# A gated linear attention and an MLP mixer on one core: queries and keys of two batches transposed by DMA, prefix sums with channels on partitions

## The chip, the core and the metric

One core of a Trainium2 chip. TensorE (PE) multiplies matrices into PSUM, which has eight banks of 128 partitions by 512 fp32 here; ScalarE (ACT) computes exponentials and copies, VectorE (DVE) elementwise operations, GpSimd (POOL) some elementwise work and the loads that change the type, and SyncE (SP) issues other transfers. Each engine runs its own queue in order and waits on semaphores for the others. The metric is the device time of one execution in microseconds; lower is better.

## The reference

The first half is an attention with a decaying state, by batch (4) and head (8), over 768 steps with a head size of 48:

```python
f = 1.0 / (1.0 + np.exp(-f_logit))
for t in range(S):
    state = f[:, :, t, :, None] * state + np.einsum('bhd,bhe->bhde', k[:, :, t], v[:, :, t])
    y[:, :, t] = np.einsum('bhd,bhde->bhe', q[:, :, t], state)
```

The second half is a mixer over the 768 steps and then over the 384 channels of `y`, with the heads put side by side as `x` (4 x 768 x 384):

```python
xt = x.transpose(0, 2, 1)
h = np.maximum(xt @ w_tok1, 0.0) @ w_tok2
u = x + h.transpose(0, 2, 1)
h2 = np.maximum(u @ w_ch1, 0.0) @ w_ch2
return (u + h2).astype(np.float32)
```

w_tok1 is 768 x 256, w_tok2 256 x 768, w_ch1 384 x 1536, w_ch2 1536 x 384. Inputs and output are float32.

## The kernel before, in words

**Attention in chunks.** A batch's 768 steps are six chunks of 128. With L = -log f, the prefix sum of L within a chunk is s; q is multiplied by exp(-s) and k by exp(s), and then the chunk is plain causal attention without a softmax, plus q times the state from the chunks before it. Steps lie on partitions, heads and channels on the free axis. In `gates` ScalarE makes L from the logits (L324, L325) and its high half as bf16 (L326), VectorE, or for batch 3 POOL, the low half (L329, L332). `attention` then does, for each chunk:

- `sums` on TensorE (L344 to L353): the prefix sums, as the triangle of ones times the high and then the low half (384 columns each), and eight matmuls of one column for the chunk's total by channel, which the last chunk doesn't need;
- two exponentials on ScalarE (L361, L363), and one of the totals (`glast`, L366);
- two products on VectorE (`qh`, L369, and `kh`, L371);
- eight transposes on TensorE of pairs of heads (L382) and one copy of the whole bank out of PSUM (`qkT`, L386), so that channels lie on partitions;
- `scores` (L396): eight matmuls with 48 contraction rows, in pairs on the upper and lower half of the array; VectorE masks them into `AmT` (L403);
- `parts` (L419): k times v for the new state, eight matmuls with 64 weight columns each, onto the upper or lower half of the partitions by the head's parity; the state is updated on VectorE (L426 to L431) and copied to a block-diagonal bf16 form, `state_bd` (L311 on ScalarE, L315 on POOL);
- `outs`: queries times the earlier state (L448) and masked scores times v (L455) in one bank, copied to `x_bf` and `x_nat`.

G, Gi, qh, kh, qkT, AmT, glast and state_bd have two buffers each, by the chunk's parity. f, k, q and v have three buffers each, by batch.

**Mixer.** For each batch `mixer` runs the token matmuls (L480, L492), adds the result into `x_nat` (L496), copies it to bf16 (`u_bf`), transposes it by 18 transposes on TensorE into six banks with six copies (`uT`, L508 and L513), and runs the channel matmuls: 72 of 384 columns for `w_ch1` (L524, each group of three followed by a relu on ScalarE or VectorE, L534 and L536), and 72 for `w_ch2` (L546), an add (L552), and an output store from SP (L555).

**Order.** Nothing is issued in the order of this text. `Plan` holds every operation with its dependencies, a rank and an estimated cost, and `order` walks through time: of all the operations that are ready it takes the one that can start first, and among equals the one of the lowest rank. That fixes the order of each engine's queue and the PSUM bank of each group; an operation that opens a bank waits for a free one. Ranks come from `due` (attention, L559) and `ranks` (mixer, L564): chunk c of batch 2 has rank 62 + 5c, of batch 3 101 + 5c; batch 2's `w_ch1` groups have 108 + 0.7n.

**Loads.** Loads on POOL keep the order in which they are written (L288 to L304, and L581): batch 0 by chunks, the four weights up to `w_ch1`, f of batch 1, chunks 0 and 1 of batch 1, `w_ch2`, the other chunks, then f, k, q and v of batch 2 whole, and of batch 3 whole. At most eight are in flight, and their rows must fit the descriptor ring.

Of the kernel before, what the change touches and what calls it, by code (L numbers as in the profile page):

```python
# [17 lines left out]
NBANK = 8  # L18
RING = 16384

# [19 lines left out]
class Plan:  # L40
# [40 lines left out]
    @staticmethod  # L81
    def cost(op, engine):

        what, *n = op.kind
        if what == "mm":
            return n[0], n[0] + 166
        if what == "el":
            free, psum, fast = n
            if engine == ACT:
                own = free / 1.2 + (67 if psum else 97)  # L90
                return own, own + 103
            if engine == DVE:
                own = free / (0.96 * fast) + 67
                return own, own + 83
            own = free * (1.2 if fast != 1.5 else 2.05) + 80
            return own, own
        return n[0], n[1]

    def order(self):
        for op in self.ops:  # L100
            first = op.before | ({op.behind} if op.behind else set())
            op.missing = len(first)
            for x in first:
                x.after.append(op)
        free = {e: 0.0 for e in (PE, ACT, DVE, POOL, SP)}
        ready = {e: [] for e in free}
        banks = [0.0] * NBANK
        wire = 0.0
        landed: list = []
        done = []  # L110

        def offer(op):
            t = max([x.end for x in op.before], default=0.0)
            if op.kind[0] == "load" and op.engines == (POOL,) and op.kind[3]:
# [3 lines left out]
                for at, rows in reversed(landed):  # L118
                    held += rows
                    if held > RING:  # L120
                        t = max(t, at)
                        break
            for e in op.engines:
                ready[e].append((t + (WAKE[e] if t else 0.0), op))

        for op in self.ops:
            if not op.missing:
                offer(op)
        while len(done) < len(self.ops):
            best = None  # L130
            for e, line in ready.items():
                for t, op in line:
                    if op.engine is not None:
                        continue
                    t = max(t, free[e])
                    if op.bank is not None and op.bank.at is None:
                        t = max(t, min(banks) + 55)
                    if best is None or (t, op.rank) < best[0]:
                        best = ((t, op.rank), e, op)
            (t, _), e, op = best  # L140
            ready[e] = [(a, o) for a, o in ready[e] if o is not op and o.engine is None]
            if op.bank is not None and op.bank.at is None:
                op.bank.at = min(range(NBANK), key=lambda j: banks[j])
                banks[op.bank.at] = math.inf
            own, till = self.cost(op, e)
            op.engine, op.start = e, t
            free[e] = t + own
            op.end = t + till
            if op.kind[0] == "load":
                size = op.kind[3]  # L150
                if size:
                    wire = max(wire, t + 1700) + size
                    op.end = wire + 1100
                if size and e == POOL:
                    landed.append((op.end, op.kind[2]))
            if op.bank is not None:
                op.bank.users -= 1
                if not op.bank.users:
                    banks[op.bank.at] = op.end
            done.append(op)  # L160
            for x in op.after:
                x.missing -= 1
                if not x.missing:
                    offer(x)
        return sorted(done, key=lambda o: o.start)
# [7 lines left out]
def kernel(  # L173
# [21 lines left out]

    sb = ctx.enter_context(tc.tile_pool(name="sb", bufs=1))
# [15 lines left out]
    q_sb = [st([128, H, NCH, D], BF16, f"q_sb{i}") for i in range(NB)]  # L212
    k_sb = [st([128, H, NCH, D], BF16, f"k_sb{i}") for i in range(NB)]
    v_sb = [st([128, H, NCH, D], BF16, f"v_sb{i}") for i in range(NB)]
    f_sb = [st([128, H, NCH, D], FP32, f"f_sb{i}") for i in range(NB)]
    Lhi = [st([128, NCH, H, 64], BF16, f"Lhi{i}") for i in range(2)]
    Llo = [st([128, NCH, H, 64], BF16, f"Llo{i}") for i in range(2)]
    G = [st([128, H, D], BF16, f"G{i}") for i in range(2)]
    Gi = [st([128, H, D], BF16, f"Gi{i}") for i in range(2)]
    qh = [st([128, H, 64], BF16, f"qh{i}") for i in range(2)]  # L220
    kh = [st([128, H, 64], BF16, f"kh{i}") for i in range(2)]
    qkT = [st([128, 8, 128], BF16, f"qkT{i}") for i in range(2)]
    AmT = [st([128, 8, 128], BF16, f"AmT{i}") for i in range(2)]
    glast = [st([128, HP], FP32, f"glast{i}") for i in range(2)]
    state = st([128, HP, D], FP32, "state")
    tsum = st([128, HP, D], FP32, "tsum")
    state_bd = [st([128, HP, 2 * D], BF16, f"state_bd{i}") for i in range(2)]
# [5 lines left out]
    uT = st([128, 3, S], BF16, "uT")  # L233
# [11 lines left out]
    names = {"f": (f_sb, f_logit), "k": (k_sb, k), "q": (q_sb, q), "v": (v_sb, v)}  # L245

    def load(what, b, c=None, engine=POOL):
        for n in what:
            dst, src = names[n]
            into = dst[b % NB] if c is None else dst[b % NB][:, :, c, :]  # L250
# [5 lines left out]
                make=[(n, b % NB, j) for j in (range(NCH) if c is None else (c,))],  # L256
# [25 lines left out]
    for i in range(2):  # L282
        for n, tl in (("L", Lhi[i]), ("L", Llo[i])):
            once(DVE, lambda tl=tl: nc.vector.memset(tl[:, :, :, D:64], 0.0), [("L", i, c) for c in range(NCH)], 400)
        for n, tl in (("qh", qh[i]), ("kh", kh[i])):
            once(DVE, lambda tl=tl: nc.vector.memset(tl[:, :, D:64], 0.0), [(n, i)], 120)
        once(DVE, lambda i=i: nc.vector.memset(state_bd[i], 0.0), [("sbd", i)], 220)
    for c in range(1, NCH):  # L288
# [10 lines left out]
    load("kqv", 1, 0)  # L299
    load("kqv", 1, 1)  # L300
    load_w("w_ch2", w_ch2, moe_w_ch2, 5600)
    for c in range(2, NCH):
        load("kqv", 1, c)
    load("fkqv", 2)  # L304
# [13 lines left out]
    def gates(b, c, r):  # L318
        fb = f_sb[b % NB][:, :, c, :]
        hi = Lhi[b % 2][:, c, :, 0:D]  # L320
        lo = Llo[b % 2][:, c, :, 0:D]
        key, lk = ("f", b % NB, c), ("L", b % 2, c)
# [12 lines left out]
    def attention(b, c, r):  # L335
        i, nb = c % 2, b % NB
        last = c == NCH - 1
        hi_c, lo_c = Lhi[b % 2][:, c], Llo[b % 2][:, c]
        lk = ("L", b % 2, c)

# [3 lines left out]
        def sums():  # L344
            pm = banks[p_s.at]
            if not last:
                bh, bl = blk(hi_c), blk(lo_c)
                for hp in range(HP):
                    g = pm[:, DM + hp:DM + hp + 1]
                    nc.tensor.matmul(g, lhsT=bh[:, hp, :], rhs=ones_bf, start=True, stop=False)  # L350
                    nc.tensor.matmul(g, lhsT=bl[:, hp, :], rhs=ones_bf, start=False, stop=True)
# [3 lines left out]
        add(PE, r, sums, need=["tri", "ones", lk], bank=p_s, kind=mms(*([1] * 8), DM, DM))  # L355

        def sview():
            return banks[p_s.at][:, 0:DM].rearrange("t (h d) -> t h d", d=D)

        el = ("el", DM, True, 1)  # L360
        add(ACT, r, lambda: nc.scalar.activation(G[i], sview(), AF.Exp, bias=0.0, scale=-1.0),  # L361
            make=[("G", i)], bank=p_s, kind=el)
        add(ACT, r, lambda: nc.scalar.activation(Gi[i], sview(), AF.Exp, bias=0.0, scale=1.0),  # L363
            make=[("Gi", i)], bank=p_s, kind=el)
        if not last:
            add(ACT, r + 1.0, lambda: nc.scalar.activation(  # L366
                glast[i], banks[p_s.at][:, DM:DM + HP], AF.Exp, bias=0.0, scale=-1.0),
                make=[("glast", i)], bank=p_s, kind=("el", 4, True, 1))
        add(DVE, r, lambda: nc.vector.tensor_tensor(qh[i][:, :, 0:D], q_sb[nb][:, :, c, :], G[i], ALU.mult),  # L369
            need=[("q", nb, c), ("G", i)], make=[("qh", i)], kind=("el", DM, False, 2))  # L370
        add(DVE, r, lambda: nc.vector.tensor_tensor(kh[i][:, :, 0:D], k_sb[nb][:, :, c, :], Gi[i], ALU.mult),  # L371
            need=[("k", nb, c), ("Gi", i)], make=[("kh", i)], kind=("el", DM, False, 2))


# [241 lines left out]
```

## Time and profile before

| what | us |
|---|---|
| median of 3 runs | 188.77 (188.32 to 189.44) |
| the profiled execution | 188.64 |
| its span on the core | 186.8 |
| granted TensorE clock | 0.997 |

Where each batch stands in the profiled execution, from the starts of single instructions (us from the span's start):

| | batch 0 | batch 1 | batch 2 | batch 3 |
|---|---|---|---|---|
| last of its loads landed (v) | 23.2 | 55.9 | 76.6 | 99.2 |
| first state formed (L426) | 10.0 | 47.3 | 81.6 | 112.9 |
| last `x_bf` | 31.7 | 73.9 | 109.0 | 148.8 |
| last `u_bf` | 36.8 | 80.6 | 117.2 | 157.6 |
| last copy of `uT` (L513) | 38.2 | 82.7 | 119.6 | 159.7 |

The second channel weight landed at 47.5, and its first matmul (L546) started at 52.56. The last channel matmul group ends at 183.4. So the stages overlap: while a batch's attention runs, TensorE also works on the channel matmuls of the batch before, and only after 162 us is one kind of work left.

The line "PE" of the page counts the time in which at least one matmul is under way; a matmul of 384 columns shows as 0.33 us though the next one starts 0.16 us after it. Times of TensorE's work are therefore read from start to start on its timeline. "idle before" names what ended an engine's wait.

### The profile page before, as it was taken

Reading aid. Unit: us, or ns where it says so; the run is one execution under the profiler, and the core shown is the slowest. Engines: PE = TensorE matmul, PEld = TensorE weight load, DVE = VectorE, ACT = ScalarE, POOL = GpSimd, SP = SyncE. Lnnn points to the kernel's source line nnn. Section 1 sums busy time; section 2 is a strip of 40 time slices with the busy share of each in tenths; the row PEclk is TensorE's granted clock in tenths of the full one; section 3 lists DMA queues with packets and bytes.
Section 4 is the critical chain, followed back from the end, with each engine's and each line's share of the span. In section 5 each row is a group of like instructions: output and inputs, shape, how many; then the busy total and the mean of one; then the engine's idle time right before and its main releaser. Section 6 shows DMA issues by size and latency. Waiting matters only on the chain.

```text
span 186.8 us, 4480 instructions
## 1 busy us (share of the span) xinstructions
PE 172.5 (92%) x1768; PEld 109.6 (59%) x1768; DVE 129.7 (69%) x295; ACT 126.9 (68%) x309; POOL 65.9 (35%) x78
## 2 busy tenths in 40 slices
PE   0589997799999999999999999999999999999992
PEld 0256664366667656676665665766666656656650
DVE  4387985749998999999988758977686638300222
ACT  4779963779983499999999935657875116698000
POOL 7999893275791444504621411011011000000000
PEclk9999999999999999999999999999999999999998
DMA  7999999999999999999992121011000121110222
GB/s 102 140 171 154 156 208 245 186 160 194 143 135 238 174 149 172 242 200 109 83 116 14 52 78 42 0 46 44 4 0 4 55 75 40 46 42 0 81 91 84
DMA packets 88437, 19.95 MB, mean 107 GB/s; under 512 B 81152, under 2 KB 87600, under 8 KB 88416
## 3 DMA queue, kind: packets, MB, share of 16 engines
q0 software_dynamic: 78720, 13.77, 91.9%
q1 hardware_dynamic: 9696, 5.90, 10.8%
q8 instruction: 14, 0.23, 0.5%
q14 instruction: 7, 0.06, 0.1%
HBM read 25.17 MB, written 4.72 MB: 160 GB/s over the span
## 4 chain that ended last, share of the span: by engine, by line
PE 84%; ACT 6%; DVE 3%; issue 2%; DMA 2%; POOL 1%; POOLq 0%; DVEq 0%; ACTq 0%
PE ps L524 26%; PE ps L546 24%; PE ps L382 7%; PE ps L480 5%; PE ps L396 4%; PE ps L492 3%; PE ps L455 3%; PE ps L419 3%; PE ps L352 2%; PE ps L508 2%; PE ps L353 2%; DMA f_sb<-in_f_logit_dram 2%; PE ps L448 2%; ACT u_bf L311 2%; ACT x_bf L311 1%
## 5 line engine op out<-in xcount | busy, mean ns | idle before, releaser
L546 PE MATMUL ps<-w_ch,zT 128*128 128x384 bf16 x288 | 54.1, 327 | 0.0
L524 PE MATMUL ps<-uT,w_ch 128*128 128x384 bf16 x288 | 52.6, 327 | 0.0
L534 ACT ACTIVATE zT<-ps 128x384 bf16<-128x384 f32 x76 | 36.5, 490 | 8.3 <-PE ps L524 7.9
L546 PEld LDWEIGHTS <-zT 128*128 128x128 bf16 x288 | 26.8, 98 | 16.5
L524 PEld LDWEIGHTS <-w_ch 128*128 128x128 bf16 x288 | 26.3, 97 | 15.9
L403 DVE TENSOR_TENSOR AmT<-ps,tri_bf 128x512 bf16<-128x512 f32 x48 | 30.6, 683 | 5.2 <-PE ps L396 5.0
L552 DVE TENSOR_TENSOR x_nat<-x_nat,ps 128x384 f32<-128x384 f32 x24 | 13.2, 550 | 22.9 <-PE ps L546 22.5
L255 POOL DMA_DIRECT2D q_sb<-in_q_dram x14 | 15.4, 1099 | 13.8 <-issue 5.7
L311 ACT ACTIVATE x_bf<-ps 128x384 bf16<-128x384 f32 x20 | 9.9, 494 | 12.9 <-PE ps L455 12.7
L255 POOL DMA_DIRECT2D k_sb<-in_k_dram x14 | 15.5, 1108 | 7.6 <-DMA f_sb<-in_f_logit_dram 4.5
L361 ACT ACTIVATE G<-ps 128x384 bf16<-128x384 f32 x24 | 11.7, 488 | 7.9 <-PE ps L353 7.8
L386 DVE COPY qkT<-ps 128x1024 bf16<-128x1024 bf16 x24 | 16.4, 685 | 0.8 <-PE ps L382 0.7
L255 POOL DMA_DIRECT2D v_sb<-in_v_dram x14 | 15.5, 1104 | 4.1 <-issue 2.5
L496 DVE TENSOR_TENSOR x_nat<-x_nat,ps 128x384 f32<-128x384 f32 x24 | 11.5, 548 | 4.1 <-PE ps L492 4.1
L311 ACT ACTIVATE u_bf<-x_nat 128x384 bf16<-128x384 f32 x24 | 11.4, 523 | 4.1 <-DVE x_nat L496 4.1
L315 POOL CAST state_bd<-state 48x192 bf16<-48x192 f32 x10 | 3.4, 343 | 29.8 <-DVE state L431 24.3
L324 ACT ACTIVATE f_sb<-f_sb 128x384 f32<-128x384 f32 x24 | 12.0, 523 | 2.7 <-DMA f_sb<-in_f_logit_dram 2.6
L480 PE MATMUL ps<-x_bf,w_tok 128*128 128x384 bf16 x48 | 12.3, 340 | 1.0 <-ACT x_bf L311 1.0
L536 DVE TENSOR_SCALAR zT<-ps 128x384 bf16<-128x384 f32 x20 | 10.4, 553 | 3.7 <-PE ps L524 3.6
L311 ACT ACTIVATE state_bd<-state 48x192 bf16<-48x192 f32 x30 | 10.8, 360 | 2.9 <-DVE state L431 2.6
L350 PE MATMUL ps<-ones_bf,Lhi 128*128 128x1 bf16 x80 | 7.0, 167 | 6.1 <-ACT Lhi L326 6.1
L326 ACT ACTIVATE Lhi<-f_sb 128x384 bf16<-128x384 f32 x24 | 12.2, 522 | 0.3
(58 smaller groups left out, 276.3 us busy)
## 6 DMA issues: line engine op xcount, KB each, us to landing
out_dram<-x_nat SPq DMA_DIRECT2D x24, 192.0 KB, 1.9
f_sb<-in_f_logit_dram POOLq DMA_DIRECT2D x3, 1152.0 KB, 11.0
f_sb<-in_f_logit_dram SPq DMA_DIRECT2D x6, 192.0 KB, 4.0
k_sb<-in_k_dram POOLq DMA_DIRECT2D x12, 96.0 KB, 6.3
q_sb<-in_q_dram POOLq DMA_DIRECT2D x12, 96.0 KB, 5.9
v_sb<-in_v_dram POOLq DMA_DIRECT2D x12, 96.0 KB, 6.0
w_ch<-in_moe_w_ch_dram POOLq DMA_DIRECT2D x2, 576.0 KB, 11.0
w_ch<-in_moe_w_ch_dram POOLq DMA_DIRECT2D x1, 1152.0 KB, 14.6
```

The source lines that it names most:

```text
L255: add(engine, 0.0, lambda eng=eng, into=into, of=of: eng.dma_start(out=into, in_=of), make=[(n, b % NB, j) for j in (range(NCH) if c is No ...
L311: nc.scalar.activation(out_, in_, AF.Copy, bias=0.0, scale=1.0)
L324: add(ACT, r, lambda: nc.scalar.activation(fb, fb, AF.Exp, bias=0.0, scale=-1.0), make=[key], kind=el)
L326: add(ACT, r, lambda: nc.scalar.activation(hi, fb, AF.Copy, bias=0.0, scale=1.0), need=[key], make=[lk], kind=el)
L382: nc.tensor.transpose(turned()[:, o + hp, :], blk(src)[:, hp, :], ident)
L386: add(DVE, r, lambda: nc.vector.tensor_copy(qkT[i], turned()), make=[("qkT", i)], bank=p_t, kind=("el", 1024, True, 2))
L403: add(DVE, r, lambda p=p: nc.vector.tensor_tensor(AmT[i][:, 4 * p:4 * p + 4, :], banks[p_a[p].at].rearrange("s (hp t) -> s hp t", t=C), tb ...
L480: add(PE, rank("tok1", rt), lambda rt=rt, kt=kt, pm=pm: nc.tensor.matmul(banks[pm.at][:, 0:DM], lhsT=w_tok1[:, kt, rt * 128:(rt + 1) * 128 ...
L524: nc.tensor.matmul(banks[pm.at][:, 0:384], lhsT=w[:, kt, c0:c0 + 128], rhs=uT[:, kt, cols], start=(kt == 0), stop=(kt == 2))
L534: nc.scalar.activation(zT[:, cc, cols], banks[pm.at][:, 0:384], AF.Relu, bias=0.0, scale=1.0)
L546: nc.tensor.matmul(banks[pm.at][:, 0:DM], lhsT=zT[:, kt, tt * 128:(tt + 1) * 128], rhs=w_ch2[:, kt, :], start=(kt == 0), stop=(kt == 11))
L552: add(DVE, rank("ch2", tt), lambda un=un, pm=pm: nc.vector.tensor_tensor(un, un, banks[pm.at][:, 0:DM], ALU.add), make=[("x_nat", xn, tt)] ...
```

## The change

For batches 2 and 3 (`TURNED`):

- q and k are transposed before the gates touch them: two transposing transfers from SP per chunk (`dma_start_transpose`, 128 steps by 512 padded channels) fill `qkT`, which has eight buffers. For this q and k lie in SBUF with heads padded from 48 to 64 channels, in two buffers by batch in place of three; f has two also.
- the prefix sums are made with channels on partitions: eight matmuls of 128 columns, the logs as weights and the triangle as the moving operand. The total is the last column of each, so the eight matmuls of one column go. The exponentials are 512 wide in place of 384, and the products on VectorE are made in place in `qkT`, 512 wide.
- the transposes on TensorE and the copy `qkT` from PSUM go.
- the state needs k with steps on partitions, so the gated k is turned back by two transposing transfers from SP per chunk, one for each parity of the heads, into `kz`, whose other parts are zero. `parts` then has 128 weight columns in place of 64, and the two heads of a pair add up in one region of PSUM.
- `u_bf` is turned by six transposing transfers from SP per batch (`TURNED_U`) in place of 18 matmuls and six copies. `uT` has another layout, for all batches, and the `w_ch1` matmuls read three runs of 128 columns.

For all batches: `w_ch2` is loaded after chunks 0 to 3 of batch 1 in place of 0 and 1 (`W2`); AmT, glast and state_bd have three buffers; the exponential for k comes before that for q; the paddings are zeroed by VectorE (`pad`), for buffer 0 at rank 30. q and k of batches 2 and 3 are loaded by chunks in place of whole, with the order f, then k and q by chunk, then v.

The planner is rewritten with indices in place of objects. It has a cost for the transposing transfers, and adds 105 ns when TensorE goes from one way of splitting the array to another. A search over random ranks is written, with zero tries.

```diff
+TURN = 105
+TRIES = 0
...
+        if what == "turn":
+            return 60 + 19 * n[0], 1900 + 20 * n[0]
...
+                    if way != mode:
+                        t = max(t, free[PE] + TURN)
+                    mode = way
...
+    TURNED = (2, 3)
+    TURNED_U = (2, 3)
+    NI, NT = 3, 8
+    W2 = 4
...
-    q_sb = [st([128, H, NCH, D], BF16, f"q_sb{i}") for i in range(NB)]
-    k_sb = [st([128, H, NCH, D], BF16, f"k_sb{i}") for i in range(NB)]
+    q_sb = [st([128, NCH, H, 64], BF16, f"q_sb{i}") for i in range(2)]
+    k_sb = [st([128, NCH, H, 64], BF16, f"k_sb{i}") for i in range(2)]
...
+    def pad(i, rank):
+        for n, tl in (("q", q_sb[i]), ("k", k_sb[i])):
+            add(DVE, rank, lambda tl=tl: nc.vector.memset(tl[:, :, :, D:64], 0.0),
+                make=[(n, i, c) for c in range(NCH)], kind=("fix", 420, 500))
+        add(DVE, rank, lambda: nc.vector.memset(kz[i], 0.0), make=[("kz", i, 0), ("kz", i, 1)], kind=("fix", 600, 700))
...
-    load("kqv", 1, 0)
-    load("kqv", 1, 1)
-    load_w("w_ch2", w_ch2, moe_w_ch2, 5600)
-    for c in range(2, NCH):
+    for c in range(NCH):
+        if c == W2:
+            load_w("w_ch2", w_ch2, moe_w_ch2, 5600)
         load("kqv", 1, c)
-    load("fkqv", 2)
...
+        if new:
+            for o, name, tl in ((4, "k", k_sb), (0, "q", q_sb)):
+                add(SP, r - 8.0, lambda o=o, tl=tl: nc.sync.dma_start_transpose(
+                    qkT[t][:, o:o + 4, :], tl[b % 2][:, c].rearrange("t h d -> t (h d)")),
+                    need=[(name, b % 2, c)], make=[("qkT", t, o)], kind=("turn", 32))
...
+            if new:
+                for hp in range(HP):
+                    a = pm[:, hp * C:(hp + 1) * C]
+                    nc.tensor.matmul(a, lhsT=bh[:, hp, :], rhs=tri_bf, start=True, stop=False)
+                    nc.tensor.matmul(a, lhsT=bl[:, hp, :], rhs=tri_bf, start=False, stop=True)
+                return
...
+        if new:
+            for o, name, tl in ((4, "Gi", Gi), (0, "G", G)):
+                add(DVE, r, lambda o=o, tl=tl: nc.vector.tensor_tensor(
+                    qkT[t][:, o:o + 4, :], qkT[t][:, o:o + 4, :], by(tl[i]), ALU.mult),
+                    need=[(name, i)], make=[("qkT", t, o)], kind=("el", wide, False, 2))
+            if not last:
+                for par in range(2):
+                    rows = slice(64 * par, 64 * par + 64)
+                    add(SP, r, lambda par=par, rows=rows: nc.sync.dma_start_transpose(
+                        kz[i][:, :, par, rows], qkT[t][rows, 4:8, :].rearrange("p hp t -> p (hp t)")),
+                        need=[("qkT", t, 4)], make=[("kz", i, par)], kind=("turn", 16))
...
+                    nc.tensor.matmul(dg()[rows, hp, :], lhsT=kz[i][:, hp, par, :] if new else kh[i][:, h, :],
+                                     rhs=v_sb[nb][:, h, c, :], start=not (new and par), stop=par == 1 or not new)
...
+        if b in TURNED_U:
+            for tt in range(NCH):
+                add(SP, rank("ut", tt), lambda tt=tt: nc.sync.dma_start_transpose(uT[:, tt], u_bf[:, tt, :]),
+                    need=[("u_bf", tt)], make=[("uT", d, tt) for d in range(3)], kind=("turn", 24))
...
-                                         rhs=uT[:, kt, cols], start=(kt == 0), stop=(kt == 2))
+                                         rhs=uT[:, 3 * th:3 * th + 3, kt, :], start=(kt == 0), stop=(kt == 2))
...
         if b == 0:
-            load("fkqv", 3)
+            pad(0, 30.0)
+        if b < 2:
+            load("f", b + 2)
+            for c in range(NCH):
+                load("kq", b + 2, c)
+            load("v", b + 2)
```

`new` is `b in TURNED`; t is the chunk's number over all batches modulo NT, i modulo 2, g modulo NI.

## The prediction

> **What bounds the kernel now.** I read the page first (busy shares, then the 40 slices), then the busy time by stage, then TensorE's timeline, then the groups by form, and last the DMA issues of the whole run and of 55 to 100 us.
>
> The page: TensorE's matmul row is busy 92% of the span. The DMA engines are full up to slice 22, about 103 us, and nearly idle after it.
>
> ```profile
> PE 172.5 (92%) x1768; PEld 109.6 (59%) x1768; DVE 129.7 (69%) x295; ACT 126.9 (68%) x309; POOL 65.9 (35%) x78
> ...
> DMA  7999999999999999999992121011000121110222
> ```
>
> A busy matmul row can hide spare time, since matmuls overlap. So I take starts: on the timeline eight 384-column matmuls from 62.76 to 64.06 are 0.162 us each, four 128-column transposes from 127.77 to 127.99 are 0.056 each, eight 48-column ones (L455, 126.52 to 126.72) and the eight single-column ones (124.67 to 124.89) 0.026 each. With these steps the matmuls of each 10 us from 40 to 180 us add up to 9.5 to 10.0 us: there is under 3 us of free TensorE time in that whole stretch. Before 40 us it is short of data (8 to 9 us are used of each 10, and far less by starts).
>
> ```profile
> core 0: us, PE busy (x) PEld busy (x) DVE busy (x) ACT busy (x) POOL busy (x), PEclk, DMA share, GB/s
> ...
> 70.00:100.00 30.00, 30.00 (x366) 19.68 (x365) 28.49 (x67) 29.13 (x76) 10.79 (x6) 1.00 1.82 146
> 100.00:162.00 62.00, 62.00 (x626) 39.63 (x625) 42.88 (x93) 36.14 (x85) 7.04 (x14) 1.00 0.10 36
> ```
>
> From 70 to 100 us VectorE and ScalarE are 95 and 97% busy too, so three engines are near their limit there; from 100 to 162 us TensorE alone is. From 162 us on only the channel matmuls of batch 3 are left.
>
> **What is taken from TensorE** (batches 2 and 3, 12 chunks, 10 of which pass on a state):
>
> ```profile
> 121.83 0.39 PE L382 MATMUL ps<-ident,qh 128*128 128x128 bf16 x4
> 122.15 0.31 PE L419 MATMUL ps<-v_sb,kh 128*64 128x48 bf16 x8
> 122.39 0.82 PE L546 MATMUL ps<-w_ch,zT 128*128 128x384 bf16 x4
> ...
> 124.89 0.32 PE L352 MATMUL ps<-Lhi,tri_bf 128*128 128x384 bf16 x1
> 125.05 0.32 PE L353 MATMUL ps<-Llo,tri_bf 128*128 128x384 bf16 x1
> 125.21 0.65 PE L524 MATMUL ps<-uT,w_ch 128*128 128x384 bf16 x3
> ...
> 126.52 0.36 PE L455 MATMUL ps<-v_sb,AmT 128*128 128x48 bf16 x8
> 126.72 0.38 PE L382 MATMUL ps<-ident,qh 128*128 128x128 bf16 x4
> ```
>
> - Transposes of q and k (L382): 12 x 8 x 0.056 = 5.4 us.
> - Transposes of u (L508): 2 x 18 x 0.056 = 2.0 us.
> - Prefix sums: 8 x 0.026 + 2 x 0.162 = 0.53 us become 8 of 128 columns, 0.45; in a last chunk 0.32 become 0.45. 10 x 0.08 - 2 x 0.12 = 0.6 us.
> - State parts (L419): 0.24 us to the next start (122.15 to 122.39), and the matmul before them is followed 0.15 instead of 0.056 us later, 0.33 in all. The new ones are 128 x 128 weights with 48 columns, as in L455: 0.21. 10 x 0.12 = 1.2 us.
>
> Sum 9.2 us, all of it in stages without free TensorE time.
>
> **What the helpers gain and lose.**
>
> ```profile
> L386 DVE COPY qkT<-ps 128x1024 bf16<-128x1024 bf16 x24 | 16.4, 685 | 0.8 <-PE ps L382 0.7
> L371 DVE TENSOR_TENSOR kh<-k_sb,Gi 128x384 bf16<-128x384 bf16 x24 | 8.5, 352 | 0.1
> L513 DVE COPY uT<-ps 128x384 bf16<-128x384 bf16 x24 | 7.0, 348 | 0.3 <-PE ps L508 0.2
> ```
>
> VectorE loses the copy of 685 ns per chunk, and its two products grow from 352 to at most 352 x 512 / 384 = 469 ns: 12 x (0.685 - 0.234) = 5.4 us less, plus 12 copies of L513, 4.2 us. New memsets: four of about 0.38 us (the size of those at L284) and two of about 0.5: 2.5 us, half before the first product at 8.6 us and half near 30 us, where VectorE is 57% busy. ScalarE's exponentials grow by 128 columns; from 4 columns at 182 ns to 384 at 490 that is 0.10 us, x 24 = 2.5 us more. Together the two engines gain, also between 70 and 100 us.
>
> **What is added to the queues.** SP gets 4 transfers per chunk (2 in a last one) and 6 per batch for u: 2 x 28 = 56, besides its 24 stores. POOL gets 24 loads of about 0.9 us for 4 of 2.2: 13 us more, where it is under half busy from 60 to 100 us; behind the loads wait POOL's Llo of batch 3 (from 90 us), which nobody needs before the first exponential of batch 3 at 110.8. The shorter rings of f, k and q cost nothing: the loads of batch 3 start at 72.7, and the last readers of batch 1 end near 68.
>
> No transposing transfer is in this trace. Nearest rows are the stores on the same queue:
>
> ```profile
> out_dram<-x_nat SPq DMA_DIRECT2D x24, 192.0 KB, 1.9
> ...
> out_dram<-x_nat SPq DMA_DIRECT2D x6, 192.0 KB, 4.5
> ```
>
> The second line is the stretch from 55 to 100 us: beside the loads a store lands after 4.5 us in place of 1.9. Three prices follow.
> (1) Latency, 1.9 us, or 4.5 while loads run. The turning of q and k has no reader waiting: it can start when a chunk of k and q lands (about 64 us; f of batch 2 lands at 62.3, the two tensors took 10.1 us for 12 chunks), against a first product at 75.9. The turning back of the gated k stands between product and state parts, but the state is needed one chunk later, 5 to 6 us on. Hidden; without that cover it is 1.9 us a chunk in batch 3, 10 us.
> (2) Time on SP per transfer: at least 0.49 us (two loads issued at 0.75 and 1.24), at most the whole time to landing, 1.9 or 4.5. I take about 0.7, nearer to the issue, since the stores at 183.30 and 183.95 show the queue free again long before a landing; 44 x 0.7 = 31 us in the 80 us that these two batches take. A transposing transfer could differ: that is the rival below.
> (3) Time on the DMA engines: 128 KB at the 160 GB/s of 55 to 100 us is 0.8 us, at the best slice's 290 GB/s 0.45. For batch 2, 12 whole and 10 half ones, 8 to 14 us, which pushes the last load (v of batch 3, landed at 99.2) to 107 to 113. The first state of batch 3 was formed at 112.9 and is wanted some 4.6 us sooner, 108. It costs 0 to 5 us of that chain; TensorE has channel matmuls of batches 1 and 2 meanwhile.
>
> A rule against the change: the Trainium skill, "VectorE: DVE Perf Modes", section "The three transpose paths", gives 1309 ns for a 128x128 bf16 transpose by DMA and 390 by TensorE, and its rules say to use TensorE where a PSUM destination will do. The trace has 56 ns a transpose in a run of them, plus the copy of 685 for eight. If 1309 ns were time on the queue, a chunk's twelve squares would hold it 15.7 us, 190 us in all, and the kernel would be much slower; if it is latency, it is the 1.9 us above. No row here tells which.
>
> **Later channel weight.** w_ch2 landed at 47.5 and is first used at 52.56. Two chunks of batch 1 (six loads, about 0.76 us apart at 48 to 53 us) go ahead: 52.1. Just in time, and those chunks give TensorE work sooner. 0 to 2 us, I take 1.
>
> **Does the end move?** Batch 3's chain must come sooner as well: from its last x_bf (148.8) to the end it is 38 us, of which 10.4 to the first channel matmul. Its chunks are ranked among the channel matmuls of batch 2, so they advance as TensorE does, and each is shorter by four transposes, a copy and a bank. u's turning takes about 2 us, as the transposes did (last u_bf 157.6, last copy 160.0), covered by L546 of batch 2. I take 1 us for waits that do not fit.
>
> Sum: 188.6 - 9.2 + 1 + 1 = 181.4. The profiled run took 188.64 (span 186.8 and 1.8 around it), 0.13 under the median, so 181.5 against 188.77. Its own range, 178.5 (no loss) to 185.
>
> **Rivals.**
> - *SP's queue becomes the bound (slower).* If a transposing transfer holds SP until it lands, 1.9 us each even when quiet, the 44 of the attention started at 64 us end at 148, with 12 stores at 0.5 us 154; one chunk's remaining chain (about 5 us) makes 159 for the last x_bf, and 38 us more 197, 199 with what is around the span. It decides from about 1.5 us per transfer: 64 + 44 x 1.5 + 6 + 5 = 141 is where the chain must be for the full gain (148.8 less 8). At 4.5 us beside the loads it would be past 210. For it: one queue, 56 transfers, fixed order, so a late store holds the ones behind it. Against: stores follow each other at 0.65 us.
> - *The gain is not passed on (no change).* The loads of batch 3 land at 113, its chunks keep their 6 us (from 110.8 to 148.8 for six), and TensorE runs out of batch 2's matmuls: 186 to 190. For it: first state at 112.9, only 3 us between first and last moment of batch 3's channel start (159.2, 162.3). Against: ranks, three sets of score buffers.
> - *The change does its work only in part:* w_ch2 late by 3 us and VectorE full at 70 to 100 us: 185.
>
> **Numbers.** A measurement of this kernel tells about 0.5%, 0.9 us, from no change. Forecast with the partial case 0.64, all faster; no gain 0.15, of it 0.04 faster, 0.08 same, 0.03 slower; SP bound 0.21, of it 0.20 slower, 0.01 same. Faster 0.68, same 0.09, slower 0.23. The range leaves out the best tenth and the far half of the SP case: 177.5 to 194.
>
> **What would show it.** Right: from 40 us to the end no TensorE gap over 0.5 us; transposing transfers landing in 2 to 5 us with issues under 1 us apart; last x_bf near 140; L546 starting by 53; VectorE near 122 us busy. Wrong: state parts or scores of batch 2 or 3 waiting on SP's transfers, issues on SP 1.5 us or more apart, TensorE idle between 100 and 160 us, or v of batch 3 landing after 115.

## The result, and the profile after

| | before | after |
|---|---|---|
| median, us | 188.55 (4 runs) | 224.78 (222.66 to 226.60, 4 runs) |
| ratio, 95% interval | 1 | 1.189 (1.176 to 1.203) |
| profiled execution, us | 188.64 | 222.66 |
| its span, us | 186.8 | 220.9 |
| granted TensorE clock | 0.997 | 0.913 |

Runs more than 1.5% above the fastest of their kernel stay out of the ratios (here 226.60), and without them the median is 223.88, which is used from here on. The kernel became 35.3 us slower; 7 us faster was forecast. First the page of the changed kernel: busy shares, the slices of TensorE, of its granted clock and of the DMA engines, the two queues with packets and megabytes, and one costly group.

```profile
PE 172.2 (78%) x1628; PEld 106.8 (48%) x1628; DVE 126.4 (57%) x283; ACT 126.6 (57%) x303; POOL 78.8 (36%) x99
...
PE   0688869999997992009998099973899899599993
...
PEclk9999995999999998556999769999589999999999
DMA  8999999999999999999999943233111121231032
...
q0 software_dynamic: 79040, 13.77, 89.3%
q1 hardware_dynamic: 33504, 11.54, 27.8%
...
L540 PE MATMUL ps<-v_sb,kz 128*128 128x48 bf16 x80 | 5.2, 194 | 27.5 <-DMA v_sb<-in_v_dram 15.1
```

TensorE has 140 matmuls fewer, yet its row has a hole of three slices at 83 to 99 us, and smaller ones later. While it stands still the granted clock (`PEclk`) falls, to 0.5 here, so what follows this stop begins slowly. The last line names the place: the matmuls of `parts` were waited for 27.5 us in all. The first column of the waits says who stands still, the second what ended the wait; then total, number and longest, all in us:

```profile
PE ps L540 <- DMA v_sb<-in_v_dram: 15.1, 1, 15.1
PE ps L540 <- DMA kz<-qkT: 12.3, 7, 6.7
...
PE ps L653 <- DMA uT<-u_bf: 4.2, 2, 2.8
```

One wait of 15.1 us for v, the others for the transposing transfers from SP: the turned-back k (`kz`) and u. The stages, as busy time of each engine, then granted clock, DMA share and GB/s (before, TensorE was busy 30.00 us of each of these three):

```profile
70.00:100.00 30.00, 13.62 (x158) 9.46 (x157) 14.20 (x31) 13.54 (x34) 5.63 (x6) 0.78 1.88 148
100.00:130.00 30.00, 22.84 (x222) 13.58 (x221) 18.86 (x44) 20.91 (x53) 13.20 (x14) 0.84 1.97 121
130.00:160.00 30.00, 24.15 (x214) 14.34 (x213) 15.97 (x33) 12.40 (x28) 3.89 (x7) 0.90 0.31 75
```

TensorE, VectorE, ScalarE and POOL are nearly idle together from 85 to 99 us, but the DMA engines are as full as before (1.88 against 1.82; the row adds up transfers that are under way together, so it passes 1), and now stay full to 130 us. What moved there, with the median time from issue to landing, for 62 to 104 us, and below it the loads of v in the same stretch before:

```profile
out_dram<-x_nat SPq DMA_DIRECT2D x5, 192.0 KB, 6.8
...
v_sb<-in_v_dram POOLq DMA_DIRECT2D x1, 576.0 KB, 31.1
qkT<-k_sb SPq DMA_TRANSPOSE x7, 7.4
qkT<-q_sb SPq DMA_TRANSPOSE x6, 7.5
kz<-qkT SPq DMA_TRANSPOSE x4, 12.7
```

```profile
v_sb<-in_v_dram POOLq DMA_DIRECT2D x2, 576.0 KB, 8.7
```

v of batch 2 was issued at 68.05 and landed at 99.16; before, it was issued at 67.42 and landed at 76.59. f of batch 3 landed at 103.2 in place of 83.7, v of batch 3 at 126.4 in place of 99.2. Part of the last is a consequence of the stop: POOL's next load stood from 81.9 to 99.5 us, and v of batch 3 was issued at 112.96 in place of 91.05. The two `kz` of the waiting chunk landed 8.3 and 11.4 us after their issue beside these loads, so they too would have held TensorE till some 96 us.

The later stops are read on SP's timeline (start, time on the queue, what):

```profile
113.76 1.22 SPq L428 DMA_TRANSPOSE qkT<-q_sb  x1
115.03 1.26 SPq L428 DMA_TRANSPOSE qkT<-k_sb  x1
116.33 1.30 SPq L428 DMA_TRANSPOSE qkT<-q_sb  x1
117.74 1.54 SPq L428 DMA_TRANSPOSE qkT<-k_sb  x1
119.37 1.31 SPq L428 DMA_TRANSPOSE qkT<-q_sb  x1
120.79 1.22 SPq L428 DMA_TRANSPOSE qkT<-k_sb  x1
122.11 3.10 SPq L483 DMA_TRANSPOSE kz<-qkT  x2
...
188.53 8.95 SPq L628 DMA_TRANSPOSE uT<-u_bf  x6
```

Each transposing transfer holds the queue for about 1.3 us, whether it is 128 x 512 (L428), half of that (L483) or 128 x 384 (L628; issues at 188.53, 189.80, 191.22, 192.54, 193.83, 195.13). The `kz` issued at 122.11 stood behind six transfers of batch 3, although its input, the gated k, was ready at 113.86; TensorE had come to its `parts` at 120.6:

```profile
113.45 0.41 DVE L477 TENSOR_TENSOR qkT<-qkT,Gi 128x512 bf16<-128x512 bf16 x1
...
119.75 0.81 PE L675 MATMUL ps<-w_ch,zT 128*128 128x384 bf16 x4
...
127.23 0.82 PE L540 MATMUL ps<-v_sb,kz 128*128 128x48 bf16 x8 [6.67 <-DMA kz<-qkT]
```

Channel matmuls stood in its queue behind `parts` (the next starts at 127.87), and could not pass.

### The profile page after: what moved, and what is told of

Same layout as the page of the kernel before. It is cut to its first block, busy times and chain, and to the rows that moved or that the text cites. A ratio compares the mean times of both kernels' runs of the same rounds, so it can differ in the third digit from the quotient of the medians.

```text
span 220.9 us, 4324 instructions
## 1 busy us (share of the span) xinstructions
PE 172.2 (78%) x1628; PEld 106.8 (48%) x1628; DVE 126.4 (57%) x283; ACT 126.6 (57%) x303; POOL 78.8 (36%) x99
## 5 line engine op out<-in xcount | busy, mean ns | idle before, releaser
L675 PE MATMUL ps<-w_ch,zT 128*128 128x384 bf16 x288 | 55.9, 335 | 0.0
L663 ACT ACTIVATE zT<-ps 128x384 bf16<-128x384 f32 x71 | 33.7, 495 | 28.7 <-DVE AmT L523 16.6
L330 POOL DMA_DIRECT2D q_sb<-in_q_dram x24 | 21.8, 908 | 26.8 <-issue 17.8
L540 PE MATMUL ps<-v_sb,kz 128*128 128x48 bf16 x80 | 5.2, 194 | 27.5 <-DMA v_sb<-in_v_dram 15.1
L330 POOL DMA_DIRECT2D k_sb<-in_k_dram x24 | 21.9, 912 | 5.5 <-DMA w_ch<-in_moe_w_ch_dram 3.8
L540 PEld LDWEIGHTS <-kz 128*128 128x128 bf16 x80 | 3.6, 102 | 30.5 <-issue 15.2
L456 ACT ACTIVATE Gi<-ps 128x384 bf16<-128x384 f32 (+1 forms) x24 | 13.2, 548 | 7.7 <-PE ps L442 4.1
L665 DVE TENSOR_SCALAR zT<-ps 128x384 bf16<-128x384 f32 x25 | 13.2, 553 | 4.8 <-PE ps L653 4.8
L620 DVE TENSOR_TENSOR x_nat<-x_nat,ps 128x384 f32<-128x384 f32 x24 | 11.9, 549 | 5.9 <-PE ps L616 5.6
L553 DVE TENSOR_TENSOR tsum<-state,ps 128x192 f32<-128x192 f32 x16 | 5.6, 348 | 13.7 <-PE ps L540 8.9
L459 ACT ACTIVATE G<-ps 128x384 bf16<-128x384 f32 (+1 forms) x24 | 13.1, 547 | 0.0
```

Source lines behind the costliest of these rows:

```text
L330: add(engine, 0.0, lambda eng=eng, into=into, of=of: eng.dma_start(out=into, in_=of), make=[(n, b % depth[n], j) for j in (range(NCH) if c ...
L456: add(ACT, r, lambda: nc.scalar.activation(Gi[i][:, 0:wide], banks[p_s.at][:, 0:wide], AF.Exp, bias=0.0, scale=1.0), make=[("Gi", i)], ban ...
L459: add(ACT, r, lambda: nc.scalar.activation(G[i][:, 0:wide], banks[p_s.at][:, 0:wide], AF.Exp, bias=0.0, scale=-1.0), make=[("G", i)], bank ...
L620: add(DVE, rank("tok2", tt), lambda un=un, pm=pm: nc.vector.tensor_tensor(un, un, banks[pm.at][:, 0:DM], ALU.add), make=[("x_nat", xn, tt) ...
L663: nc.scalar.activation(zT[:, cc, cols], banks[pm.at][:, 0:384], AF.Relu, bias=0.0, scale=1.0)
L665: nc.vector.tensor_scalar(zT[:, cc, cols], banks[pm.at][:, 0:384], 0.0, None, ALU.max)
```

## Theories

*Loads made late:* the transposing transfers of batch 2 take so much of the full DMA engines that batch 2's last load comes 22 us late, and TensorE's fixed order stops at it. *SP's queue:* 1.3 us a transfer, in an order planned at half that or less, makes `kz` late whatever the loads do. *The rest of the change* (rings, load order, planner, later `w_ch2`) costs time by itself.

## Experiments: which part

"Frame" is the changed kernel with nothing turned by transfers. Each is compared with runs of the kernel before on the same chip (medians 188.55 to 189.08).

**Frame.**

```diff
-    TURNED = (2, 3)
-    TURNED_U = (2, 3)
+    TURNED = ()
+    TURNED_U = ()
```

> No batch is turned by transfers: neither q and k of batches 2 and 3 nor u; all the rest of the change stays (shorter rings of f, k and q, k and q of batches 2 and 3 loaded by chunks with v behind them, w_ch2 later, three score buffers, the paddings, the planner's 105 ns). Theory A (the transposing transfers and the loads slow each other on the DMA engines, and the static order then stops TensorE behind one late load): 187 to 190 us, as before the change. Theory B (each transposing transfer holds SP's queue 1.3 us and lands 2.3 us later, the same in both batches): also 187 to 190. Theory C (the frame itself costs: loads by chunks, v last, w_ch2 late): 194 us or more.

192.69 us, ratio 1.022 (1.016 to 1.029): 4 of the 35 us come without a transposing transfer. Two runs split this. With `W2 = 2`, the old place of `w_ch2`:

> The frame alone (nothing turned by transfers) with w_ch2 loaded after chunks 0 and 1 of batch 1, as before the change. If the later channel weight costs the frame's 4 us: 187.5 to 190. If it costs nothing: 191.5 to 194, and the rest of the frame is the cause.

194.24, ratio 1.030 (1.022 to 1.037): the later load does not cost; by the medians it gains 1.5 us, though the two intervals overlap. With `TURN = 0`, so that the planner adds nothing for another way of splitting the array:

> The frame with the planner's cost of another splitting of the array set from 105 ns to 0. If this cost, through the order that it leads to, is what makes the frame slower than the kernel before: 187.5 to 190 us. If not: 191.5 to 194 us.

189.98 (8 runs), ratio 1.006 (1.003 to 1.010): most of the frame's cost, 2.7 us, is the order that the planner makes with this term.

**Batch 3 alone, batch 2 alone, u alone** (`TURNED = (3,)`, `TURNED = (2,)`, or only `TURNED_U = (2, 3)`).

> q and k of batch 3 alone are turned by transfers, u not. Theory A: the transfers meet only the last loads, so little is lost: 183 to 192 us. Theory B: half of the 22 attention transfers' price in each batch: some 200 to 206 us. Theory C: as without any turning, 194 or more.

> q and k of batch 2 alone are turned by transfers, u not. Theory A: nearly the whole loss stays, since these run beside the loads of v of batch 2 and all of batch 3: 205 to 215 us, with v of batch 2 landing after 90 us. Theory B: like batch 3 alone, 200 to 206 us, with v of batch 2 landing near 80. Theory C: 194 or more.

> u of batches 2 and 3 alone is turned by transfers, q and k not. Theory A: u is turned after the last load, so it costs no loads; TensorE saves 2.0 us and may wait about 1 to 3 us per batch for the transfers: 186 to 191 us. Theory B: six transfers of 1.3 us in a row and 2.3 to land, against 2 us for the transposes, 6 us later per batch, of which batch 3's counts in full: 192 to 196 us. Theory C: 194 or more.

| turned | us | ratio | against the frame | v of batch 2 / 3 landed |
|---|---|---|---|---|
| q, k of batch 3 | 191.52 | 1.016 (1.008 to 1.023) | -1.2 | 78.1 / 109.5 |
| q, k of batch 2 | 206.63 | 1.096 (1.086 to 1.105) | +13.9 | 98.1 / - |
| u of both | 194.06 | 1.027 (1.019 to 1.035) | +1.4 | - |
| all | 223.88 | 1.189 (1.176 to 1.203) | +31.2 | 99.2 / 126.4 |

The waits of TensorE with batch 2 alone:

```profile
PE ps L540 <- DMA v_sb<-in_v_dram: 15.0, 1, 15.0
...
PE ps L540 <- DMA kz<-qkT: 2.3, 4, 0.9
```

Batch 2 alone brings the whole 15 us stop. With batch 3 alone v of batch 3 is late by 10 us as well, but nobody stands waiting for it, and nothing is lost against the frame. The parts do not add up: 13.9 - 1.2 + 1.4 is 14, not 31. One thing that only the runs with both batches have is a long stop for `kz`, 6.7 us at 120 in the changed kernel: there a `kz` of batch 2 stands behind the transfers of batch 3. With either batch alone no wait of TensorE's matmuls for `kz` is over 0.9 us. This stop is not the whole of the missing 17 us.

Without u's turning but with both batches (`TURNED_U = ()`):

> The changed kernel without the turning of u (18 transposes on TensorE again in batches 2 and 3), q and k of both batches turned by transfers. The two batches alone cost +14 (batch 2) and -1 us (batch 3) over the frame. If they add up: 205 to 208 us, and the rest of the changed kernel's 224.8 is u's. If batch 3's transfers are what suffers from batch 2's late loads (both in one queue of SP): 216 to 223 us.

Two runs, 216.34 and 221.28: the transfers for u are the smaller part, some 3 to 8 us of the 35, which two runs that lie 5 us apart do not tell better. Batch 3 alone with the old place of `w_ch2`:

> q and k of batch 3 alone turned by transfers, u not, and w_ch2 loaded as early as before the change. It takes 3 us of work from TensorE and meets few loads. If w_ch2 is the frame's cost: 186 to 189 us, faster than the kernel before by up to 1%. If not: 190.5 to 193.

193.76, ratio 1.027 (1.021 to 1.033), 2.2 us more than with the new place: the same sign a second time.

## Experiments: the transfers by themselves

The kernel before gets twelve transfers that nobody reads, on SP, from 63 us on, in the place of batch 2's turning of q and k.

```diff
+    tz = st([128, 512], BF16, "tz")
+    tq = [st([128, 4, 128], BF16, f"tq{i}") for i in range(8)]
...
+        for i in range(12):
+            add(SP, 50.0, lambda i=i: nc.sync.dma_start_transpose(tq[i % 8], tz),
+                need=["tz", key], make=[("tq", i % 8)], kind=("fix", 650, 2000))
```

> The kernel before the change, with twelve transposing transfers of 128 x 512 bf16 added on SP as soon as f of batch 2 has landed (62 us). Nobody reads what they write. Theory A (contention on the DMA engines, about 1.3 us of all engines for each): v of batch 2 lands at 88 to 94 us in place of 76.6, and TensorE waits for it: 195 to 204 us. Theory B (only the queue and the latency cost, where somebody reads the result): loads land as before within 2 us, and the time is that of before, 187 to 190 us.

The second form copies the same 128 KB without transposing (`dma_start`); the third was meant to put the transposing ones after the last load.

> The same, with twelve plain transfers of the same 128 KB in place of the transposing ones, at the same place. Theory A with the bytes as the price (0.5 us each): v of batch 2 lands at 80 to 84 us, 188 to 192 us in all. If a transposing transfer costs the engines no more than a plain one, this run equals the one with transposing transfers; if transposing itself is the price, this run is near the kernel before.

> The same twelve transposing transfers, started when the last load (v of batch 3, 99 us) has landed. Both theories: no load is left to slow, nobody waits, 187 to 190 us. Their spacing on SP and their time to landing in a quiet stage are read from the trace: 1.3 us and 2.3 us are expected from the changed kernel's trace after 135 us.

Issues between 62 and 104 us, transposing and then plain:

```profile
v_sb<-in_v_dram POOLq DMA_DIRECT2D x2, 576.0 KB, 15.4
tq<-tz SPq DMA_TRANSPOSE x12, 7.6
```

```profile
tq<-tz SPq DMA_DIRECT2D x12, 128.0 KB, 5.4
v_sb<-in_v_dram POOLq DMA_DIRECT2D x2, 576.0 KB, 11.5
```

| twelve transfers | us | ratio | v of batch 2 / 3 landed |
|---|---|---|---|
| none (before) | 188.55 to 189.08 | 1 | 76.6 / 99.2 |
| transposing | 204.15 | 1.079 (1.069 to 1.089) | 91.1 / 109.9 |
| plain | 196.78 | 1.040 (1.027 to 1.053) | 83.6 / 102.0 |
| transposing, at 78 to 98 us | 189.81 (8 runs) | 1.004 (1.000 to 1.009) | - / 111.8 |

By the last load of all, twelve transposing transfers cost the loads 10.6 us, 0.9 each; in the third run 12.6, or 1.05 each; plain ones 2.8, 0.23 each. By v of batch 2, which was under way beside them, it is 14.5 and 7.0 us, so the ratio of the two kinds is between two and four. In time the plain ones cost 7.8 us against 15.1: about half of the loss comes with the bytes at this place, the other half with transposing them. SP had plain ones 0.6 to 0.75 us apart and transposing ones 1.5 to 1.7 beside the loads. The third did not wait for the loads: only the planned order stood against an earlier start, and so the twelve ran at 78 to 98 us beside batch 3's loads. It shows something else: a delay of 12.6 us in the last load cost nothing (0.4%, at the edge of what can be told) where no reader stands at it: v of batch 3 landed at 111.8, and before the first state of that batch was formed at 112.9.

The first run's 15.1 us are more than its stop for v, which is 6.6 us. A second load had a reader in front of it: f of batch 3 landed at 96.5, before at 83.7, and ScalarE, which works in order too, stood at the first step of its gates for 10.5 us. In the plain run f landed at 88.9, and this wait is 3.7 us, with no stop for v (both from 70 to 130 us):

```profile
ACT f_sb L334 <- DMA f_sb<-in_f_logit_dram: 10.5, 1, 10.5
...
ACT f_sb L334 <- DMA f_sb<-in_f_logit_dram: 3.7, 1, 3.7
```

TensorE then waited for ScalarE's `glast`, 2.3 us and 3.0. Busy time and granted clock of the first run at 80 to 90 and 90 to 100 us:

```profile
80.00:90.00 10.00, 4.20 (x60) 3.17 (x57) 5.88 (x17) 5.11 (x15) 2.22 (x1) 0.93 1.69 181
90.00:100.00 10.00, 6.08 (x53) 3.73 (x52) 4.41 (x10) 3.23 (x9) 4.43 (x2) 0.50 2.13 182
```

TensorE is idle for 9.7 of these 20 us, and what it does from 90 to 100 it does at half the clock, another 3 us by estimate. This stop cost more than its length.

## Experiments: order of the loads, and loads nearly gone

**v ahead of k and q.** If only v's place in the line were wrong, this would mend it.

```diff
             load("f", b + 2)
+            load("v", b + 2)
             for c in range(NCH):
                 load("kq", b + 2, c)
-            load("v", b + 2)
```

> The changed kernel with v of batches 2 and 3 loaded ahead of their k and q instead of behind. If the 15 us stop at 84 us comes from v being last in the line of loads while transposing transfers slow that line: v of batch 2 lands near 69 us, the stop goes, and the time falls to 203 to 212 us, while q and k land later and the last load (now q of batch 3) still lands after 115 us. If the stop comes from elsewhere (SP's queue, TensorE's order), little changes: 220 to 228 us.

222.41 (two runs), ratio 1.175 (1.163 to 1.187), within 1% of the changed kernel: the expected gain is missing. v of batch 2 landed at 68.8, and TensorE stopped at the same place, now for `kz`:

```profile
PE ps L540 <- DMA kz<-qkT: 29.1, 13, 17.4
```

SP reached that `kz` at 93.86, behind the transfers of the last chunks, one of which held the queue for 8.2 us from 78.39 on (the trace does not say why), while the k and q of the last landed only at 89.4 and 90.8. In these two orders the delay belongs to the stream of transfers and loads as a whole, and the order says who carries it.

**Light loads.** Loads of batches 2 and 3 bring one head of eight, with the same instructions in the same order on TensorE, ScalarE and SP (one memset more on VectorE); seven eighths of these batches' input is left out.

```diff
+            if b >= 2:
+                into, of = into[:, 0:1], of[:, 0:1]
...
+    once(DVE, lambda: nc.vector.memset(v_sb[2], 0.0), [("v", 2, c) for c in range(NCH)], 1200)
```

> The changed kernel with every transposing transfer in place and the same order on TensorE, ScalarE, VectorE and SP, but with loads of batches 2 and 3 that bring one head of eight (the other heads keep older data, so seven eighths of those batches' input are left out; one memset of v's third buffer is added). Theory A (transposing transfers and loads slow each other on the DMA engines): the 15 us stop at 84 us goes, and with it what follows: 178 to 190 us, as predicted for the change. Theory B (the transfers' time on SP's one queue and their latency on the chain): the order and the queue are the same, so most of the loss stays: 205 us or more.

> The same light loads, with nothing turned by transfers: the base for the light kernel, as the frame (192.7 us) is for the changed one. Loads did not hold the frame's TensorE after 40 us, so both theories: 189 to 193 us. The light kernel less this one is what the transposing transfers are worth where no loads are beside them; by the prediction -6 to -9 us.

**Measured prices in the planner**, with whole loads and, in the second, with light ones (same order on TensorE and SP in both; a list of dependencies is sorted besides):

```diff
-            return 60 + 19 * n[0], 1900 + 20 * n[0]
+            return 1300, 2400
...
-                late = min(max(wire - t - 1000, 0), 2600)
-                wire = max(wire, t + 1500) + 16 * op.kind[1]
+                late = max(wire - t - 1000, 0)
+                wire = max(wire, t + 1500) + 30 * op.kind[1]
```

> The changed kernel, planned anew with the prices that the runs so far showed for a transposing transfer: 1.3 us on SP and 2.4 us to landing for each, 0.96 us of the DMA engines for 128 KB and no limit on how late it gets behind the loads (in place of 0.67 us, 2.5 us, 0.51 us and at most 2.6 us late). If the loss comes from an order that was made for transfers too cheap, TensorE meets its waits later and fills them with channel matmuls: 200 to 212 us. If the transfers as such are too many for the stage, whatever the order: 215 to 226 us.

> The light loads (one head of eight in batches 2 and 3) with the order that the measured prices of a transposing transfer gave (TensorE's and SP's order as in the run g1_prices). If what is left of the loss under light loads (207.0 against 191.6) comes from the order, made for transfers of 0.36 to 0.67 us on SP that hold it 1.3: 188 to 197 us. If 56 transfers of 1.3 us and 2.3 us of latency are too many for the chain in any order: 203 to 208 us.

| | whole loads | light loads |
|---|---|---|
| changed kernel | 223.88, 1.189 | 205.7, 1.091 (1.081 to 1.102) |
| with measured prices | 214.53 (212.85 and 216.20) | 198.0, 1.046 (1.042 to 1.049) |
| frame | 192.69, 1.022 | 191.62, 1.016 (1.010 to 1.021) |

Waits of TensorE with light loads and the old prices, and below them the transfers of 62 to 104 us:

```profile
PE ps L543 <- DMA kz<-qkT: 14.2, 11, 4.0
...
PE ps L656 <- DMA uT<-u_bf: 4.4, 2, 2.7
```

```profile
qkT<-k_sb SPq DMA_TRANSPOSE x8, 3.4
qkT<-q_sb SPq DMA_TRANSPOSE x8, 3.3
kz<-qkT SPq DMA_TRANSPOSE x8, 2.3
```

The wait for v is gone, transfers land in 2.3 to 3.4 us, and `kz` still stops TensorE 11 times, 14.2 us in all: this comes from SP's queue and the 2.3 us to landing, in an order that was planned for cheaper transfers. With measured prices no wait of TensorE's matmuls for `kz` is left, 7.7 us are gained, and TensorE's busy time at 70 to 100 us goes from 25.19 to this:

```profile
70.00:100.00 30.00, 28.41 (x298) 18.51 (x297) 28.61 (x64) 26.71 (x66) 5.20 (x7) 1.00 0.57 94
```

Still 6.4 us more than the light frame, though TensorE has some 8 us less to do; after 40 us none of its waits there is over 1.6 us, so no single stop carries them. With whole loads the planner's prices gain some 8 to 11 us by the two runs, and one stop of 11.9 us for v of batch 2 stays.

## Experiment: a version to beat both

Batch 3 alone, `TURN = 0`, no turning of u; then the same with measured prices.

> q and k of batch 3 alone turned by transfers, u not, and no 105 ns in the planner. The frame gained 2.7 us from the latter; if that holds here too: 187.5 to 190 us, about the kernel before. If the order differs otherwise: 190.5 to 192.5 us.

> The same with the measured prices of a transposing transfer in the planner. Batch 3's stops for kz were 2.5 us in all (0.7 to 1.1 each); planned for, they can be filled with channel matmuls: 186 to 189 us. If the planner's prices make no difference: as without them.

189.70 (12 runs), ratio 1.004 (1.001 to 1.007), and 189.04 (12 runs), ratio 0.999 (0.996 to 1.001): no better than the kernel before. No version beat it.

## Why the prediction was wrong

**Where the 35.3 us are**, from medians: frame 192.69 - 188.55 = 4.1; transfers with light loads 205.7 - 191.6 = 14.1, of which 7.7 go with measured prices in the plan; whole in place of light loads 223.9 - 205.7 = 18.2; less 192.7 - 191.6 = 1.1, which the loads cost the frame too. 4.1 + 14.1 + 18.2 - 1.1 = 35.3. Light loads also leave the transfers more room, so the 18.2 is what loads and transfers cost together, not a delay of one load alone.

- *TensorE's savings: right.* By an estimate from the counts of matmuls and their start-to-start steps its work fell by 7.9 us, from 158.9 to 151.0, against 9.2 forecast, and the new sums follow each other at 0.056 us as assumed. But by the same estimate TensorE's free time from 40 us on grew from about 3 to about 43 us, half-rate time after stops included.
- *Helpers: right in that they hold nothing up, VectorE's gain half of the forecast.* It was busy 126.4 us after 129.7, 122 was forecast; five more of the relus went to it (2.8 us). The longest stop of TensorE's matmuls for it from 40 us on is 1.1 us.
- *Price (3), time on the DMA engines: the step that failed, twice.* First the size: 0.45 to 0.8 us for 128 KB, by the GB/s of other loads. The runs with twelve unread transfers show a delay of 0.9 to 1.2 each in the stretch where the loads keep the engines full, two to four times that of a plain transfer of these bytes (0.23 to 0.58). Second, and worse, the load it was charged to: what "pushes the last load", v of batch 3, "costs 0 to 5 us of that chain". That v did come late (126.4, above the 115 named as the sign), but in the run with batch 3 alone a delay of 10 us there cost nothing. v of batch 2, last in its batch's line, for which I named no delay, came 22.6 us late, and TensorE stood in front of it for 15.1 us. The cover that the price leaned on, "TensorE has channel matmuls of batches 1 and 2 meanwhile", was not there: TensorE takes its queue in order, and what stood behind the waiting `parts` could not start.
- *Price (2), time on SP: mis-sized.* 0.7 us was taken from plain stores; 1.27 to 1.42 us was measured from issue to issue in quiet (u's six), about the same for the other sizes, and up to 2 beside loads. The 1309 ns of the Trainium skill ("VectorE: DVE Perf Modes", "The three transpose paths") agrees with the time on the queue of a whole transfer of up to four squares, not with that of each square, and not with the latency, which was 2.3 to 2.4 us in quiet.
- *Price (1), "hidden": failed for `kz` and u.* The latency itself was near the forecast in quiet (2.3 for 1.9). What was left out is the place in SP's line: a `kz` behind six transfers of the next batch is issued 8 us after its input is ready, and TensorE's queue gave no cover, whatever work stood behind the waiting instruction. With light loads these waits are 14.2 us for `kz` and 4.4 for u. Of the signs named against the forecast three came in full: `parts` waiting on SP's transfers, TensorE idle between 100 and 160 us, v of batch 3 after 115. Issues on SP 1.5 us or more apart came too, but beside loads and not as the rule.
- *Later channel weight: right in sign.* It landed at 53.4 (52.1 forecast), its first matmul started at 55.2 (by 53 forecast), and it gains 1.5 to 2.2 us by the medians (1 forecast), with intervals that overlap both times. *The planner's 105 ns* was not in the sum; it costs 2.7.
- *The rivals.* SP's queue as the bound (199, "decides from about 1.5 us per transfer") came nearest to 14 of the 35 us, at a price below its own threshold: the sum of the queue's time had room, and single late transfers stopped TensorE all the same. Since 7.7 of the 14 go with another order, it was not the bound that the rival describes. No rival had a load of batch 2 made late by transfers that were issued before it was finished. The range ended at 194.

Still open: why v of batch 2 took 31 us when f of batch 3, issued behind it, landed only 4 us after it; the trace does not split a transfer over the 16 engines. The frame's last 1.3 us have no named place, nor have the 6.4 us that are left with light loads and measured prices. Transposing transfers from another engine's queue were not tried, nor were they held by a dependency until the loads were over.

## What to carry to other kernels

Before a transfer is added, look at the DMA slices of the stretch in which it will run: where they are full, as here, the loads under way pay for it, and the question is who stands in front of each of them in a fixed order. Price a transfer of a new kind with unread copies of it in the old kernel: twelve of them cost 15 us here. Busy time that is taken from a full engine is worth nothing if each of its in-order instructions gets a new thing to wait for.

## What the hardware showed that I had not expected

- A transposing transfer keeps SP's queue about 1.3 us for 128 x 512, 64 x 512 and 128 x 384 alike in the changed kernel; a plain one of 128 KB 0.6 to 0.75, in the run with plain transfers.
- Beside loads that fill the DMA engines, the unread transposing transfers landed after 5.6 to 9.0 us, those of the changed kernel after up to 15.2 us, against 2.3 to 2.4 in quiet. From 70 to 90 us the load queue of the changed kernel moved 0.94 MB, where before it moved 2.90, while SP's queue moved 2.04 in place of 0.62: together 3.0 MB in place of 3.5 from engines that were full in both.
- The granted clock fell with the stop and came back late: 1.00 up to 85 us, 0.67 from 85 to 90, 0.50 from 90 to 100, 0.63 from 100 to 105, 1.00 from 105 to 110, though TensorE was busy again from 99.3.
